# Narrowing float64 weights: the low three bits from ScalarE instead of VectorE

## The chip, the cores and the metric

One core of a Trainium2 chip runs the whole program in one launch. The metric is the device time of that core in microseconds (us), taken as the median of several runs.

## The reference

The reference computes attention, then two gated layers (MoE 1 and MoE 2), in float32 from float32 q, k and v and weights given in float64:

```python
# attention: q, k, v of (4, 8, 576, 64); pooled by 4 tokens, plus a band |i - j| < 4
x = out_up + out_local                      # 2304 tokens x 512
x = (sigmoid(x @ w_gate) * (x @ w_val)) @ w_out      # 512 -> 1536 -> 512
h = x @ w_in                                         # 512 -> 2048
out = (h * tanh(softplus(h))) @ w2_out               # 2048 -> 512
```

The weights arrive as 8-byte float64 words. The kernel has to turn each into a float32 word before it can use it.

## The kernel before, in words

The work runs batch by batch (four batches of 576 tokens). `block(b, extra)` (L910) lays out the matrix products of MoE 1 for batch b, and `weave` (L792) puts the steps of the weights, of the next batch's attention and of the MoE 2 weights among them, each when its due time on a TensorE clock has come. The first batch is different: its attention steps stand in an order written out by hand (`ORDER`, L20 to L30), with the engine of each step in `ENG` (L32 on). A scheduler then fixes the order of the instructions on each engine. After the fourth batch MoE 2 follows (L1051 on).

TensorE multiplies in pairs of float32r words: every float32 operand is split by `split` (L189) into a high part (ScalarE, L190) and a low part (POOL for the first batch's weights, VectorE for others, L191). The products of MoE 1 are at L857 to L859 (gate and value) and L888 to L892 (out), those of MoE 2 at L1060 to L1062 and L1068 to L1070. `m1` evaluates the gate with a tanh on ScalarE (L862) and a product on VectorE (L863).

The weights of MoE 1 come in 18 units of two pieces each. For batch 0 a piece is loaded raw as 128 x 512 float64 words by `load64` (L169; SP queue, L171; two buffers of the tag "raw"), made float32 by `narrow` (L176), and split. A narrowed unit lies in a tile `d` (two buffers) and is also written to DRAM (`wd`, L228 and L256), from where the later batches load it ready-made (L219). Units 0 to 2 are steps of the hand-written order (`wf`, `wn`, `ws`); the others go through `part` (L242), each load being put behind the step of the piece before. The 32 pieces of the MoE 2 weights go through `narrow_steps` (L944) during batches 1 to 3, into a single-buffered tile `d2`.

So `narrow` runs 36 times in the first batch and 32 times later. For one piece it does this:

- L178, ScalarE: the high word of each float64, read as a float32, times 2^-112, into `g` ("rebias"). It subtracts the exponent bias and keeps the 11 lower exponent bits and the top 20 bits of the fraction in place.
- L180, VectorE: `d = g << 3`.
- L181, VectorE: `d = (low word >> 29) | d`, the last three fraction bits.
- L185, VectorE: `d = (g & sign bit) | d`.

L181 is the last reader of the raw buffer, L185 the last reader of `g`, and L180 the first writer of `d`. Attention's own rows that appear below are L98 (copies), L414 (evictions of transposed tokens), L481 and L605 (exponentials), L586 (mask), L636 (normalisation), L648 and L664 (transposes and products), L674 (joining the two attentions).

Of the kernel before, what the change touches and what calls it, by code (L numbers as in the profile page):

```python
# [9 lines left out]
F32R = mybir.dt.float32r  # L10
I32 = mybir.dt.int32
AF = mybir.ActivationFunctionType
ALU = mybir.AluOpType
# [3 lines left out]
SIGN = -2147483648  # L17
# the first batch's loads and steps in the order of their issue
ORDER = [['k0a', 'k0c', 'k1a', 'k1c', 'q0a', 'q0c', 'v1a', 'v1c', 'w0', 'q1c', 'v0c', 'w2', 'v0a',
# [11 lines left out]
# the engines of those steps, and how far apart the second batch's steps are laid (ns)  # L31
ENG = {'L.t0': 3000, 'L.t': 420, 'L.vd': 3750, 'L.vd0': 1800, 'L.pool': 1600, 'L.ls': 4500, 'L.s1':  # L32
# [16 lines left out]
def attn_moe_kernel(  # L49
# [13 lines left out]
    PE, DVE, ACT, POOL, SP = nc.tensor, nc.vector, nc.scalar, nc.gpsimd, nc.sync  # L63
# [18 lines left out]
    scale = 1.0 / float(D) ** 0.5  # L82
# [3 lines left out]
    def subs(b):  # L86
        """The two parts of the tokens of batch b that the products of MoE 1 take in turn."""
        a = 2 * TQ if b == 0 else SUB
        return slice(0, a), slice(a, S)
# [10 lines left out]
    class Step:  # L100
        """A piece of a program: what emits it, the time it takes of the tensor engine, and
        what has to lie how far back on the tensor engine's clock."""

# [3 lines left out]

    # ---------------------------------------------------------------- memory
    const = ctx.enter_context(tc.tile_pool(name="const", bufs=1, side="left"))
# [19 lines left out]
    xl = R[:, OX + NX:OX + 2 * NX].rearrange("p (c t) -> p c t", c=KD)  # L129
    # the products of MoE 1 come to lie where the first batch's rows are gone  # L130
    first = tc.alloc_tile_pool(name="first", bufs=1, side="left", reuse_waits="tile")
# [12 lines left out]
    for n in range(B * NU1):  # L144
        i = n % NRING
        slot_of[n] = (OR + i * 2048, user.get(i))
        user[i] = n
    last = slot_of[B * NU1 - 1][0]
# [18 lines left out]

    # ------------------------------------------------- float64 words to float32
    def load64(src, n):  # L169
# [6 lines left out]
    def narrow(r, d):  # L176
        g = fpool.tile([128, 512], F32, tag="rebias", name="rebias")
        ACT.activation(out=g, in_=r[:, :, 1].bitcast(F32), func=AF.Copy, scale=2.0 ** -112)  # L178
        gi, di = g.bitcast(I32), d.bitcast(I32)
        DVE.tensor_scalar(out=di, in0=gi, scalar1=3, scalar2=None, op0=ALU.logical_shift_left)  # L180
        DVE.scalar_tensor_tensor(  # L181
            out=di, in0=r[:, :, 0], scalar=29, in1=di,
            op0=ALU.logical_shift_right, op1=ALU.bitwise_or,
        )
        DVE.scalar_tensor_tensor(  # L185
            out=di, in0=gi, scalar=SIGN, in1=di, op0=ALU.bitwise_and, op1=ALU.bitwise_or
        )
# [4 lines left out]

    # ------------------------------------------------------- weights of MoE 1
    def src1(u, x):
# [14 lines left out]
    def weights(b):  # L209
        """The steps that bring the units of block b on chip and split them."""  # L210
        steps = []
# [74 lines left out]

    # ------------------------------------------------------------- attention
    class St:
        pass

    def windows(i):
        """Of tile i: first query, first key, first row used and rows used, for its halves."""
        q0, n = tiles[i]
        got = []
        for z in range(2):
            want, m = q0 + z * QH, min(QH, n - z * QH)
            first = min(want, S - WK)
            got.append((first, min(max(want - 3, 0), S - WK), want - first, m))
        return got

    def attention(b):
# [42 lines left out]

        # the first batch's rows lie where the products of MoE 1 come later, four neighbouring
        # tokens of half the sequence to a partition
        def load_rows(src, nm, half, a):
# [108 lines left out]

        # pooled attention, half the queries at a time; heads in the order (parity, pair)
        def g_scores(qh, h0):
# [37 lines left out]

        # the same for half of the pairs, with the transposes
        def f_norm(qh, p0):
# [66 lines left out]

        # banded attention, two windows of 64 queries by 64 keys at a time
        def l_scores(i, e):
# [224 lines left out]
    def weave(slots, steps):  # L792
        """Emits the slots in their order, and the steps among them: each once what it stands
        on lies far enough back, and the paced ones evenly by cost."""
        slots, steps = list(slots), list(steps)
        total_s = sum(z.cost for z in slots) or 1.0
        total_e = sum(z.cost for z in steps if z.paced) or 1.0
        at_s = at_e = 0.0

        def ready(z):  # L800
            t = 0.0
            for name, lat in z.deps:
                if name not in done_at:
                    return None
                t = max(t, done_at[name] + lat)
            return t

        while slots or steps:
            pick, soonest = None, None
            for z in steps:  # L810
                t = ready(z)
                if t is None:
                    continue
                if t <= clock[0]:
                    if z.cost and z.paced and slots and at_e / total_e > (ENG["PACE"] if ("slot", 0, NU1 - 1) not in done_at else 1.15) * at_s / total_s + 0.01:
                        continue
                    pick = z
                    break
                soonest = t if soonest is None else min(soonest, t)
            if pick is None and slots:  # L820
                t = ready(slots[0])
                if t is not None and t <= clock[0]:
                    pick = slots.pop(0)
                    at_s += pick.cost
                elif t is not None:
                    soonest = t if soonest is None else min(soonest, t)
            elif pick is not None:
                steps.remove(pick)
                if pick.paced:
                    at_e += pick.cost  # L830
            if pick is None:
                assert soonest is not None
                clock[0] = soonest
                continue
            pick.fn()
            clock[0] += pick.cost
            done_at[pick.name] = clock[0]

    # ----------------------------------------------------------------- MoE 1
    late = []  # L840
# [5 lines left out]
    def m1(b, f, sub):  # L846
# [13 lines left out]
        sg = fpool.tile([128, SUBM], F32, tag="sg", name="sg")  # L860
        # sigmoid(a) = (1 + tanh(a / 2)) / 2; the last half comes with the second product
        ACT.activation(out=sg[:, 0:n], in_=ps[0][:, 0:n], func=AF.Tanh, scale=0.5)  # L862
# [12 lines left out]
    def m1out(b, c2, fg, j, ps):  # L875
# [19 lines left out]
        if fg == last_g:  # L895
            if b == B - 1 and c2:
                # the ring is free but for its last unit
                a = free_at[j // 2] + j % 2 * 1024
                t = R[:, a:a + 2 * n].rearrange("p (z t) -> p z t", z=2)
            else:  # L900
                t = stage(n)
# [8 lines left out]
    def block(b, extra):  # L910
        """MoE 1 of batch b with the steps of `extra` woven in."""
        slots = []
# [27 lines left out]

    # ------------------------------------------------------- weights of MoE 2
    w2raw = {}

    def narrow_steps(tag, srcs, first, use, gap):  # L944
        """Steps that turn the pieces `srcs` (source, rows) to float32 and hand them to `use`,
        one each `gap` from `first` on."""
        steps = []
# [23 lines left out]
    if True:  # L971
        make_identity(nc, ident)
        POOL.memset(mask, 0.0)
        # row r of a half and column j: queries lie 0 or 3 keys after their window's first
        for z, offs in enumerate(((0, 3), (3, 3), (3, 0))):
# [71 lines left out]

        # ------------------------------------------------------------- MoE 2
        at.release()
# [21 lines left out]

        # tanh(softplus(h)) = n / (n + 2) = n/2 * exp(-ln(n/2 + 1)) with n = e^h (e^h + 2);
        # from h = 10 on it is 1 in float32, and the minimum keeps n in range
        tc.keep_in_program_order(ACT.preload_act_table_set("natural_log_exp_and_others"))
# [30 lines left out]
        for t in range(NT2):  # L1105
# [17 lines left out]
            if t > 0:  # L1123
                for a in range(2):
                    finish(t - 1, po[a], a, full)
        # the last tile's output comes in pieces, so that little is left behind the last product
        for a, cs in ((0, full), (1, slice(0, DM // 2)), (1, slice(DM // 2, DM))):
# [38 lines left out]
```

## Time and profile before

| what | value |
|---|---|
| runs, median of 3 | 1075.83 us (1075.07 to 1077.99) |
| profiled execution, span from its first to its last instruction | 1069.6 us |
| TensorE (PE) busy | 1023.1 us, 96% |
| VectorE (DVE) busy | 690.6 us, 65% |
| ScalarE (ACT) busy | 521.3 us, 49% |
| POOL busy | 195.2 us, 18% |
| moved by DMA | 134.51 MB, mean 126 GB/s |

The span leaves out what lies ahead of the first instruction and behind the last; the profiled execution has no time of its own beside the span, so the span is set against the median of the runs, which is 6.2 us more. The shares are averages over very different stages: POOL has nearly all of its work in the first quarter, and VectorE is far busier there than later. In rows of instructions a number in square brackets is the idle time of the engine just before, with what ended it.

### The profile page before, as it was taken

What the parts mean: (1) busy time and instruction counts of PE and PEld (TensorE: products, weight loads), DVE (VectorE), ACT (ScalarE), POOL (GpSimd) and SP (SyncE); (2) the same over time, 40 slices, a digit from 0 to 9 for tenths busy, and PEclk for the clock granted to TensorE, in tenths of its full rate; (3) what the DMA queues carried; (4) which work ended last, traced back from release to release, by engine and by line L of the source; (5) the groups of instructions that cost most, each with busy time, mean ns of one, the idle gap of its engine ahead of it and who ended that gap; (6) DMA issues with size and microseconds to landing.
All of it is one profiled execution on the core that took longest, in us unless ns stands there. A gap on an engine that the chain in (4) does not pass through costs nothing.

```text
span 1069.6 us, 20453 instructions
## 1 busy us (share of the span) xinstructions
PE 1023.1 (96%) x8152; PEld 956.0 (89%) x8152; DVE 690.6 (65%) x1107; ACT 521.3 (49%) x1222; POOL 195.2 (18%) x235
## 2 busy tenths in 40 slices
PE   4698988999999999999999999999999999999998
PEld 3588978899999999899999999999999999999997
DVE  6977988856975537955488931867555555555552
ACT  4654657346665437565356631654443443433432
POOL 6456564630400400400000002000000000000000
PEclk9998998999999999999999999999999999999999
DMA  8639665777752457622375548212112020220001
GB/s 199 174 103 238 178 204 189 220 241 237 220 184 60 135 179 227 212 101 61 124 243 182 173 167 264 65 29 59 23 37 60 1 60 5 56 60 1 21 1 40
DMA packets 122240, 134.51 MB, mean 126 GB/s; under 512 B 54432, under 2 KB 99488, under 8 KB 122144
## 3 DMA queue, kind: packets, MB, share of 16 engines
q1 hardware_dynamic: 110336, 115.37, 35.1%
q0 software_dynamic: 11808, 17.83, 6.2%
q8 instruction: 64, 1.05, 0.4%
q14 instruction: 32, 0.26, 0.1%
HBM read 101.19 MB, written 31.98 MB: 124 GB/s over the span
## 4 chain that ended last, share of the span: by engine, by line
PE 77%; DVE 11%; DMA 6%; ACT 3%; issue 2%; SPq 0%; POOL 0%; DVEq 0%; ACTq 0%
PE ps_m L857 7%; PE ps_m L859 7%; PE ps_m L858 7%; PE h L1060 6%; PE h L1062 6%; PE h L1061 6%; PE po L1070 6%; PE po L1068 6%; PE po L1069 6%; PE ps_o L888 5%; PE ps_o L890 4%; PE ps_o L892 4%; DVE d L181 2%; DMA raw<-in_moe_w_out_dram 2%; DVE d L185 2%
## 5 line engine op out<-in xcount | busy, mean ns | idle before, releaser
L857 PE MATMUL ps_m<-R 128*128 128x288 f32 (+2 forms) x768 | 236.0, 309 | 4.2 <-DVE sg L863 4.2
L858 PE MATMUL ps_m<-R 128*128 128x288 f32 (+2 forms) x768 | 232.5, 303 | 0.8 <-POOL R L191 0.8
L859 PE MATMUL ps_m<-R 128*128 128x288 f32 (+2 forms) x768 | 232.7, 303 | 0.5 <-POOL R L191 0.5
L857 PEld LDWEIGHTS ps_m<-R 128*128 128x128 f32 x768 | 148.4, 194 | 9.6 <-DVE sg L863 4.6
L190 ACT CAST R<-d 128x512 fp32r<-128x512 f32 (+1 forms) x192 | 108.6, 583 | 89.2 <-PE ps_o L890 34.4
L858 PEld LDWEIGHTS ps_m<-R 128*128 128x128 f32 x768 | 148.8, 194 | 1.9 <-POOL R L191 1.0
L859 PEld LDWEIGHTS ps_m<-R 128*128 128x128 f32 x768 | 148.6, 194 | 1.7 <-POOL R L191 0.9
L191 DVE TENSOR_TENSOR R<-d,R 128x512 fp32r<-128x512 f32 (+1 forms) x158 | 105.5, 682 | 55.1 <-ACT R L190 52.9
L888 PE MATMUL ps_o<-G,R 128*128 128x288 f32 (+2 forms) x384 | 116.5, 303 | 0.0
L890 PE MATMUL ps_o<-G,R 128*128 128x288 f32 (+2 forms) x384 | 114.4, 298 | 0.0
L892 PE MATMUL ps_o<-G,R 128*128 128x288 f32 (+2 forms) x384 | 114.2, 298 | 0.0
L1068 PE MATMUL po<-R,G 128*128 128x512 f32 (+1 forms) x247 | 94.5, 383 | 0.0
L1069 PE MATMUL po<-R,G 128*128 128x512 f32 (+1 forms) x247 | 94.0, 381 | 0.0
L1070 PE MATMUL po<-R,G 128*128 128x512 f32 (+1 forms) x247 | 93.5, 383 | 0.0
L1081 ACT ACTIVATE e<-e 128x1024 f32<-128x1024 f32 (+1 forms) x48 | 40.6, 846 | 107.2 <-DVE e L1080 107.2
L1062 PE MATMUL h<-R 128*128 128x256 f32 x320 | 90.2, 282 | 0.0
L1061 PE MATMUL h<-R 128*128 128x256 f32 x320 | 90.2, 282 | 0.0
L1060 PE MATMUL h<-R 128*128 128x256 f32 x320 | 90.2, 282 | 0.0
L1080 DVE TENSOR_SCALAR e<-h 128x1024 f32<-128x1024 f32 (+1 forms) x48 | 45.9, 956 | 58.3 <-PE h L1062 58.1
L178 ACT ACTIVATE rebias<-raw 128x512 f32<-128x512 f32 x68 | 46.0, 677 | 59.8 <-DMA raw<-in_moe_w_out_dram 23.5
L888 PEld LDWEIGHTS ps_o<-G,R 128*128 128x128 f32 x384 | 72.9, 190 | 1.2
L890 PEld LDWEIGHTS ps_o<-G,R 128*128 128x128 f32 x384 | 73.0, 190 | 0.1
(126 smaller groups left out, 2290.3 us busy)
## 6 DMA issues: line engine op xcount, KB each, us to landing
d<-wd SPq DMA_DIRECT2D x54, 512.0 KB
raw<-in_moe_w_out_dram SPq DMA_DIRECT2D x28, 512.0 KB
wd<-d SPq DMA_DIRECT2D x18, 512.0 KB
wd<-R SPq DMA_DIRECT2D x32, 256.0 KB
raw<-in_moe_w_in_dram SPq DMA_DIRECT2D x16, 512.0 KB
x2d<-R SPq DMA_DIRECT2D x24, 288.0 KB
R<-wd POOLq DMA_DIRECT2D x13, 512.0 KB, 6.9
raw<-in_moe_w_gate_dram SPq DMA_DIRECT2D x12, 512.0 KB
```

The source lines that it names most:

```text
L857: PE.matmul(p[:, 0:n], lhsT=wh, rhs=xh[:, c, ts], start=(c == 0), stop=False)
L858: PE.matmul(p[:, 0:n], lhsT=wh, rhs=xl[:, c, ts], start=False, stop=False)
L859: PE.matmul(p[:, 0:n], lhsT=wl, rhs=xh[:, c, ts], start=False, stop=(c == KD - 1))
L888: PE.matmul(p[:, 0:n], lhsT=hi[:, o:o + 128], rhs=gt[:, f, 0, ts], start=(f == 0), stop=False)
L890: PE.matmul(p[:, 0:n], lhsT=hi[:, o:o + 128], rhs=gt[:, f, 1, ts], start=False, stop=False)
L892: PE.matmul(p[:, 0:n], lhsT=lo[:, o:o + 128], rhs=gt[:, f, 0, ts], start=False, stop=(f == KF1 - 1))
L1060: PE.matmul(o, lhsT=wi[:, 0, c, cs], rhs=x[:, 0, c, :], start=(c == 0), stop=False)
L1061: PE.matmul(o, lhsT=wi[:, 0, c, cs], rhs=x[:, 1, c, :], start=False, stop=False)
L1062: PE.matmul(o, lhsT=wi[:, 1, c, cs], rhs=x[:, 0, c, :], start=False, stop=(c == KD - 1))
L1068: PE.matmul(p, lhsT=g[:, 0, ts], rhs=w[:, 0, cs], start=(j == 0), stop=False)
L1069: PE.matmul(p, lhsT=g[:, 0, ts], rhs=w[:, 1, cs], start=False, stop=False)
L1070: PE.matmul(p, lhsT=g[:, 1, ts], rhs=w[:, 0, cs], start=False, stop=(j == KF2 - 1))
```

## The change

A second ScalarE instruction makes the low three bits. It reads one byte of each float64, the highest byte of the low word, computes byte / 32 + 1 / 64 - 1 / 2 and writes it as an int32 into `d`; the conversion rounds to the nearest whole number, which is byte >> 5. VectorE then does `d = (g << 3) | d` and, as before, `d = (g & sign bit) | d`. L180 is gone, L181 no longer reads the raw words, and the first writer of `d` and the last reader of the raw buffer are now one ScalarE instruction. The remaining hunks of the diff only take away comments.

```diff
+U8 = mybir.dt.uint8
...
     def narrow(r, d):
         g = fpool.tile([128, 512], F32, tag="rebias", name="rebias")
         ACT.activation(out=g, in_=r[:, :, 1].bitcast(F32), func=AF.Copy, scale=2.0 ** -112)
         gi, di = g.bitcast(I32), d.bitcast(I32)
-        DVE.tensor_scalar(out=di, in0=gi, scalar1=3, scalar2=None, op0=ALU.logical_shift_left)
+        ACT.activation(
+            out=di, in_=r.bitcast(U8)[:, :, 3], func=AF.Copy, scale=1.0 / 32, bias=1.0 / 64 - 0.5
+        )
         DVE.scalar_tensor_tensor(
-            out=di, in0=r[:, :, 0], scalar=29, in1=di,
-            op0=ALU.logical_shift_right, op1=ALU.bitwise_or,
+            out=di, in0=gi, scalar=3, in1=di, op0=ALU.logical_shift_left, op1=ALU.bitwise_or
         )
         DVE.scalar_tensor_tensor(
             out=di, in0=gi, scalar=SIGN, in1=di, op0=ALU.bitwise_and, op1=ALU.bitwise_or
         )
```

## Rows read from the trace of the kernel before

**Rows 1.** Stages: stretch, length, busy us of PE, PEld, DVE, ACT, POOL; granted clock, DMA.
```profile
0.00:28.00 28.00, 13.28 (x128) 10.59 (x128) 18.77 (x39) 12.32 (x37) 17.61 (x44) 1.00 0.85 200
28.00:60.00 32.00, 24.00 (x214) 20.64 (x215) 29.83 (x49) 17.85 (x55) 13.17 (x12) 1.00 0.72 197
60.00:220.00 160.00, 144.89 (x1379) 134.34 (x1378) 134.57 (x217) 89.97 (x270) 101.16 (x104) 0.94 0.63 184
220.00:1070.00 850.00, 840.93 (x6435) 790.42 (x6433) 507.48 (x804) 401.14 (x864) 63.30 (x77) 1.00 0.35 110
```

**Rows 2.** Chain that ended last, 28 to 220 us, shares of the stretch by line.
```profile
by line: DVE d L181 8.9%; DVE d L185 7.7%; DMA raw<-in_moe_w_val_dram 6.8%; DVE d L180 6.5%; issue 5.8%; DMA raw<-in_moe_w_out_dram 5.5%; PE ps_m L858 4.2%; PE ps_m L859 4.0%; PE ps_m L857 4.0%; DMA raw<-in_moe_w_gate_dram 3.8%; DMA vw<-in_
```

**Rows 3.** TensorE's timeline: start, length, instruction, wait before it with what ended it.
```profile
42.66 1.96 PE L664 MATMUL ps_la<-ETl,vw 64*64 64x58 f32 x32 [1.86 <-ACT ETl L97]
...
97.99 1.12 PE L579 MATMUL ps_l<-kT,qT 64*64 64x64 f32 x16 [2.35 <-ACT qT L414]
...
176.69 0.50 PE L555 MATMUL ps_ga<-ETg,vd 72*64 72x72 f32 x2 [2.21 <-DVE El L586]
...
198.94 1.14 PE L664 MATMUL ps_la<-ETl,vw 64*64 64x58 f32 x32 [1.73 <-issue]
...
219.18 0.63 PE L648 MATMUL ps_lt<-ident,El 128*128 128x128 f32 x4 [2.15 <-DVE El L636]
...
291.34 0.40 PE L857 MATMUL ps_m<-R 128*128 128x288 f32 x1 [1.93 <-DVE sg L863]
```

**Rows 4.** A short stretch behind one of those waits, columns as in rows 1.
```profile
98.00:104.80 6.80, 6.80 (x40) 6.16 (x40) 4.00 (x9) 5.97 (x24) 5.29 (x9) 0.51 1.07 262
```

**Rows 5.** VectorE's groups at L180, to 60, 60 to 220, after 220 us.
```profile
L180 DVE TENSOR_SCALAR d<-rebias 128x512 int32<-128x512 int32 x6 | 6.5, 1078 | 0.3 <-ACT rebias L178 0.3
...
L180 DVE TENSOR_SCALAR d<-rebias 128x512 int32<-128x512 int32 x30 | 21.5, 720 | 13.4 <-ACT rebias L178 7.9 <-POOL R L191 4.1 <-issue 1.3
...
L180 DVE TENSOR_SCALAR d<-rebias 128x512 int32<-128x512 int32 x32 | 17.4, 543 | 2.0 <-ACT rebias L178 1.8
```

**Rows 6.** Shortest, median and longest of a kind (ns); the last gives its mean.
```profile
L180 DVE TENSOR_SCALAR d<-rebias x68: 409/426/2216, 30.8 to 609.2; 128x512 int32<-128x512 int32 x68
...
L178 ACT ACTIVATE rebias<-raw x68: 652/676/705, 30.1 to 605.4; 128x512 f32<-128x512 f32 x68
...
L190 ACT CAST R<-d x34: 601/618/647, 35.4 to 217.5; 128x512 fp32r<-128x512 f32 x34
...
L1081 ACT ACTIVATE e<-e 128x1024 f32<-128x1024 f32 (+1 forms) x48 | 40.6, 846 | 107.2 <-DVE e L1080 107.2
```

**Rows 7.** SP queue's waits to 225 us: total, times, longest.
```profile
SPq L171 <- DVE d L181: 70.4, 26, 7.7
```

**Rows 8.** One piece's timeline, from its rebias to the next load into its raw buffer.
```profile
37.16 0.67 ACT L178 ACTIVATE rebias<-raw 128x512 f32<-128x512 f32 x1 [1.08 <-DMA raw<-in_moe_w_gate_dram]
...
40.05 0.69 DVE L181 SCALAR_TENSOR_TENSOR d<-raw,d 128x512 int32<-128x512 int32 x1
...
40.82 0.37 SPq L171 DMA_DIRECT2D raw<-in_moe_w_gate_dram  x1
```

**Rows 9.** VectorE's timeline at three places ahead of TensorE's waits.
```profile
93.85 2.95 DVE L185 SCALAR_TENSOR_TENSOR d<-rebias,d 128x512 int32<-128x512 int32 x1
...
173.48 1.50 DVE L180 TENSOR_SCALAR d<-rebias 128x512 int32<-128x512 int32 x1
...
290.51 0.41 DVE L180 TENSOR_SCALAR d<-rebias 128x512 int32<-128x512 int32 x1
```

**Rows 10.** ScalarE's timeline at two places.
```profile
96.83 0.62 ACT L190 CAST R<-d 128x512 fp32r<-128x512 f32 x1 [3.23 <-DVE d L185]
...
209.78 0.67 ACT L178 ACTIVATE rebias<-raw 128x512 f32<-128x512 f32 x1 [3.53 <-DMA raw<-in_moe_w_out_dram]
```

**Rows 11.** POOL's timeline at unit 15's second split.
```profile
211.96 1.28 POOL L191 TENSOR_TENSOR R<-d,R 128x512 fp32r<-128x512 f32 x1
```

**Rows 12.** VectorE's waits to 225 us: total, times, longest.
```profile
DVE d L180 <- POOL R L191: 4.1, 1, 4.1
```

## The prediction

> **What bounds the kernel now.** I read the stages first [rows 1]. TensorE is busy 840.93 of 850 us after 220 us: there it is the bound, and work on VectorE or ScalarE can hide. Before that it stands idle for 14.7 us (to 28), 8.0 us (28 to 60) and 15.1 us (60 to 220). The first narrowing starts at 30 us [rows 6], so the first 14.7 us are out of the change's reach. From 60 to 220 us the granted clock is 0.94 in the mean: 0.06 x 160 = 9.6 us of TensorE time are lost to it. One of four such falls shows where: right behind the 2.35 us wait that ends at 97.99 [rows 3] the granted clock is 0.51 for 6.8 us [rows 4], the lower of its two levels (1.2 GHz instead of 2.4), which costs half of that, 3.4 us. So at most 8.0 + 15.1 + 9.6 = 32.7 us can be won before 220 us.
>
> Next the chain of waits over these 192 us [rows 2]. The three narrowing lines of VectorE hold 8.9 + 7.7 + 6.5 = 23.1% of it, L180 alone 6.5%, or 12.5 us; raw weight loads hold 6.8 + 5.5 + 3.8 = 16.1%, or 31 us; the three MoE 1 products only 12%. VectorE is busy 29.8 of 32 and 134.6 of 160 us, ScalarE 17.9 and 90.0 [rows 1]. So the early stage hangs on VectorE's queue and on the ring of raw loads behind it, and ScalarE has room in the mean. The reader should see in TensorE's timeline [rows 3] that its waits are for attention steps (a mask, a copy, a normalisation) that stand in VectorE's or ScalarE's queue behind narrowing, rarely for weights themselves.
>
> **The change, part by part.** *VectorE loses L180.* In the first batch that is 6 of 1.078 and 30 of 0.720 us, 6.5 + 21.5 = 28.0 us; later 32, 17.4 us [rows 5]. Its shortest is 0.409, its longest 2.216 us [rows 6]: the surplus is waiting that falls into the instruction, so the 36 are worth between 36 x 0.409 = 14.7 and 28.0 us. L181 only gets another input of the same size; I take its duration as unchanged.
>
> The rows show L180 drawn out to 1.50 us at 173.48, and L185, which stays, to 2.95 us at 93.85 [rows 9]; so what draws one out can also draw out the other. I therefore use neither total for the gain, but credit it below wait by wait. The Trainium skill's page "SBUF — State Buffer", section "Who interferes with whom", speaks against the larger number: VectorE and GpSimd hold one shared port pair exclusively for a whole instruction, and an instruction with two SBUF inputs is blocked as well, so the wait would pass from L180 to its successor. L185's 2.95 us agrees with that; by the rule VectorE is relieved of 14.7 us, by the rows' means of 28.0.
>
> *ScalarE gains one instruction per piece.* Its kind (byte in, int32 out) is not in the trace. The nearest row is L178: same 512 elements, same distance of 8 bytes, same function, 0.676 us [rows 6]. A plain cast of as many neighbouring words takes 0.618, one of 1024 elements 0.846 [rows 6]; that bounds it. I take 0.676, or 36 x 0.676 = 24.3 us in the first batch (22.2 to 30.5). ScalarE's 120.1 us of the first 220 become 144, 66%. The 32 later ones, 21.6 us, hide behind TensorE at 99% with ScalarE at 401 of 850; without that cover they would cost up to their 21.6 us.
>
> *A piece's own latency grows.* VectorE's first operation now needs both ScalarE results: with idle engines 0.676 takes the place of 0.409, 0.27 us more per piece. This is covered while the raw loads are waited for.
>
> *The raw buffer comes free sooner.* The load queue waits 70.4 us in 26 waits for L181 [rows 7]. For one piece rebias starts at 37.16, L181 ends at 40.74 and the load goes out at 40.82 [rows 8]. Now the second ScalarE instruction ends at 37.16 + 2 x 0.676 = 38.5, so the load can leave 2.3 us sooner. SP's queue is in order, so the token and value loads behind it move up too; no DMA is added. What is late next is then ScalarE or POOL's split.
>
> *The first write of d moves to ScalarE.* Its wait for the buffer goes with it; priced among the rivals.
>
> *What of this reaches TensorE.* 28 to 60 us: the load that leaves 2.3 us sooner feeds the piece behind which the next attention steps queue, and the wait of 1.86 us at 42.66 [rows 3] is for a copy behind a narrowed piece: I credit 2.5 of the 8.0 us idle, less than the two together (4.2) because ScalarE is nearly without gaps around 30 to 36 us. 60 to 220 us: the wait before 97.99 comes of L185's 2.95 us, which held a ScalarE cast for 3.23 us [rows 9, 10] and a copy behind it; both operations of that piece would now be through before, worth 2.35 + 3.4 with the clock, of which I credit 3.5. The wait before 176.69 ends in a mask operation behind L180's 1.50 us: 1.0 of 2.21. Before 219.18 two L180 stand in the way: 1.0 of 2.15. Before 198.94, 0.7 of 1.73; for all others together 1.3. That is 7.5 us, 0.27 of the 28.0 us taken from VectorE. The ScalarE instructions delay what stands behind them: 30 x 0.676 = 20.3 us, about half of it while ScalarE is busy (90 of 160 us), and at the same 0.27 it costs 2.7, say 2.5 us. After 220 us: twice, before 291.34 and once more near 442, TensorE waits for a gate product that stands right behind an L180 of 0.41 us [rows 3, 9]: 0.7 us. Sum: -2.5 - 7.5 + 2.5 - 0.7 = **-8.2 us**, span 1069.6 to 1061.4; the median of the runs lies 6.2 us above the span, so 1075.8 - 8.2 = **1067.6 us**.
>
> **Rivals.** *Larger gain.* With the loads sooner and VectorE relieved, the long waits go and the clock stays up from 60 to 220 us: 9.6 + 7.5 + 2.5 + 0.7 = 20 us without the ScalarE charge, and with part of it 1055 to 1062, middle 1059. For it: the falls stand behind waits of one to two and a half microseconds. Against: VectorE and POOL stay the same crowded pair.
>
> *No change.* What draws L180 out beyond its shortest only passes to the next VectorE operation, so the relief is 14.7 instead of 28.0 us and the credit 7.5 x 14.7 / 28.0 = 3.9 us; with the early 2.5 halved and ScalarE's charge at its upper bound (2.5 x 30.5 / 24.3 = 3.1) about -2.8 is left: 1073 to 1078, middle 1075. Against: L180's share of the chain. The Trainium skill's rule on the shared port pair ("SBUF — State Buffer", "Who interferes with whom") comes out here.
>
> *Slower: the write in place stops ScalarE.* The byte instruction needs a free d buffer, and thus POOL's split of the unit two back. Before, VectorE waited for that once, 4.1 us [rows 12], at unit 17: its rebias ended at 210.45, the split at 213.24 [rows 10, 11], so ScalarE would stand 2.8 us, with tanh, exponentials and evictions behind it. As loads come 2.3 us sooner, other units get there too. Three such waits of 2 us on TensorE, each with a fall of the clock (9.6 us over four falls, 2.4 each), are 3 x 4.4 = 13.2; less half of the gain, 4, this gives +9, 1085. It decides once ScalarE reaches a unit's byte instruction over 1 us before POOL is through. Against: only one such wait so far.
>
> The order of each queue is the scheduler's and may come out differently; a few microseconds either way, within these ranges.
>
> **How the numbers follow.** About 0.3%, 3.2 us, can be told from no change. Forecast 0.45 (1062 to 1072.6), larger gain 0.17, no change 0.15, slower 0.23. Faster 0.45 + 0.17 = 0.62, same 0.15, slower 0.23. The range takes in the larger gain down to 1057 and the slower case up to 1083; beyond lie some 0.06 and 0.11. The likeliest case's own range is 1062 to 1073.
>
> **What would show it.** Right: L180's group gone, the byte instruction near 0.68 us; SP's waits for VectorE at L171 gone and much less than 70 us left; VectorE's busy time to 220 us down by 15 to 28 us; TensorE idle from 28 to 220 us down from 23.1 to some 17 us, and fewer falls of the clock. Wrong: L185 and its neighbour growing by as much as L180 gave up (no change); ScalarE waiting for POOL ahead of the byte instruction, and TensorE's waits now put down to ScalarE (slower); or a byte instruction well over 0.85 us.

## The result, and the profile after

The changed kernel takes 1082.55 us (median of 4 runs, 1081.76 to 1085.68) against 1075.45 us for the kernel before: a ratio of 1.0092, 95% interval 1.0066 to 1.0118. It is slower by 0.9%, where 0.8% faster was forecast. The profiled execution took 1083.0 us, with a span of 1081.2 us, 11.6 more than before. Lines from `narrow` on stand 4 further down: rebias L179, the byte instruction L183, VectorE's two operations L186 and L189, the casts L194, POOL's split L195.

TensorE's busy time rose from 1023.1 to 1028.0 us, and its idle time from 1069.6 - 1023.1 = 46.5 to 1081.2 - 1028.0 = 53.2. So 6.7 of the 11.6 us are waits and 4.9 are the same products taking longer. The stages of the changed kernel, with the columns of [rows 1], show where:

```profile
0.00:28.00 28.00, 13.28 (x128) 10.59 (x128) 18.11 (x39) 11.66 (x33) 16.82 (x43) 1.00 0.86 193
28.00:60.00 32.00, 24.99 (x235) 21.39 (x237) 27.60 (x53) 24.38 (x76) 14.90 (x15) 1.00 0.75 207
60.00:220.00 160.00, 147.85 (x1369) 137.08 (x1370) 115.77 (x178) 102.71 (x289) 99.81 (x104) 0.90 0.61 178
220.00:240.00 20.00, 12.90 (x98) 12.51 (x97) 5.01 (x9) 6.75 (x13) 5.51 (x6) 0.74 0.78 244
220.00:1081.00 861.00, 841.88 (x6424) 790.06 (x6422) 493.93 (x771) 418.63 (x895) 60.74 (x76) 0.99 0.36 109
```

What the change was to bring did come. VectorE is busy for 18.1 + 27.6 + 115.8 = 161.5 us to 220 us, 21.7 less than in [rows 1]; TensorE's idle time from 28 to 220 us fell from 23.1 to 7.0 + 12.2 = 19.2 us. But the granted clock of 60 to 220 us went from 0.94 to 0.90, and the stretch behind it, where TensorE had not waited, now has 7.1 us of idle time in 20, and a clock of 0.74. Before, that stretch was:

```profile
220.00:240.00 20.00, 20.00 (x172) 19.72 (x171) 9.47 (x15) 7.95 (x17) 6.59 (x7) 1.00 0.78 256
```

VectorE's two remaining operations from 60 to 220 us, behind the two that they replace, and SP's waits to 225 us (total, times, longest), answer to [rows 5, 7]:

```profile
L185 DVE SCALAR_TENSOR_TENSOR d<-rebias,d 128x512 int32<-128x512 int32 x30 | 28.9, 968 | 0.3
L181 DVE SCALAR_TENSOR_TENSOR d<-raw,d 128x512 int32<-128x512 int32 x30 | 26.3, 882 | 0.2
...
L189 DVE SCALAR_TENSOR_TENSOR d<-rebias,d 128x512 int32<-128x512 int32 x30 | 28.4, 958 | 0.2
L186 DVE SCALAR_TENSOR_TENSOR d<-rebias,d 128x512 int32<-128x512 int32 x30 | 26.3, 884 | 13.7 <-ACT d L183 13.5 <-ACT rebias L179 0.2
```

```profile
SPq L172 <- ACT d L183: 39.2, 15, 14.7
SPq L260 <- DVE d L189: 24.5, 7, 4.9
SPq L329 <- POOL vd L432: 13.9, 7, 3.9
```

Three of TensorE's waits between 90 and 240 us (start, length, instruction, and in brackets the wait before it):

```profile
95.41 0.68 PE L583 MATMUL ps_l<-kT,qT 64*64 64x64 f32 x16 [1.91 <-ACT qT L418]
...
154.06 1.16 PE L668 MATMUL ps_la<-ETl,vw 64*64 64x58 f32 x32 [1.97 <-ACT od L565]
...
230.30 1.96 PE L668 MATMUL ps_la<-ETl,vw 64*64 64x58 f32 x32 [7.10 <-ACT ETl L98]
```

At each the clock fell, right behind the first two and during the third, as it did behind the wait of [rows 4], but for longer. The columns are those of [rows 1]:

```profile
96.70:106.90 10.20, 9.35 (x49) 8.47 (x49) 6.53 (x12) 8.91 (x30) 5.29 (x6) 0.52 1.06 239
154.70:175.20 20.50, 20.50 (x127) 18.18 (x124) 10.17 (x22) 9.10 (x25) 3.72 (x4) 0.51 0.47 150
226.40:236.60 10.20, 6.30 (x50) 6.20 (x51) 3.07 (x6) 5.52 (x12) 2.50 (x2) 0.52 0.87 315
```

The 7.10 us wait is new, and two timelines tell how it comes about. First ScalarE, then SP:

```profile
227.41 0.66 ACT L179 ACTIVATE rebias<-raw 128x512 f32<-128x512 f32 x1 [9.73 <-DMA raw<-in_moe_w_out_dram]
...
229.66 0.59 ACT L98 COPY ETl<-ps_lt 128x512 f32<-128x512 f32 x1
```

```profile
213.50 7.38 SPq L329 DMA_DIRECT2D araw<-in_v_dram  x4
220.97 0.83 SPq L172 DMA_DIRECT2D raw<-in_moe_w_out_dram  x2
```

The copy that TensorE needs stands behind the rebias of the first MoE 2 piece; that rebias waits 9.73 us for its raw load; and the raw loads stand on SP's queue behind four loads of attention values, which wait in turn for POOL to free their buffer. Nothing of this is `narrow`. In the kernel before, the raw loads went out at 215.90 and the same copy ran at 221.94 us:

```profile
215.90 0.95 SPq L171 DMA_DIRECT2D raw<-in_moe_w_out_dram  x2
...
221.94 0.58 ACT L97 COPY ETl<-ps_lt 128x512 f32<-128x512 f32 x1
```

The order on the queues had changed, and not only here. The program hands its work to the scheduler in the same order as before, yet of the instructions that both kernels have, some 60 of SP's 369, 160 of TensorE's 7320, 160 of ScalarE's 1020 and 190 of VectorE's 1039 stand elsewhere, by the two lists that the last experiment writes out. So two theories stood against each other: **A**, the loss comes from the new order of the queues; **B**, it comes from the new instruction on ScalarE itself.

### The profile page after: what moved, and what is told of

Its sections match the earlier page's. It is cut to its first block, busy times and chain, and to the rows that moved or that the text cites. A ratio compares the mean times of both kernels' runs of the same rounds, so it can differ in the third digit from the quotient of the medians.

```text
span 1081.2 us, 20349 instructions
## 1 busy us (share of the span) xinstructions
PE 1028.0 (95%) x8152; PEld 959.1 (89%) x8152; DVE 655.4 (61%) x1039; ACT 557.4 (52%) x1290; POOL 192.3 (18%) x235
## 4 chain that ended last, share of the span: by engine, by line
PE 71%; DMA 10%; DVE 8%; ACT 6%; issue 3%; POOL 1%; SPq 0%; ACTq 0%; DVEq 0%; POOLq 0%
PE h L1064 6%; PE h L1066 6%; PE h L1065 6%; PE po L1074 6%; PE po L1072 6%; PE po L1073 6%; PE ps_o L892 5%; PE ps_m L861 5%; PE ps_o L894 4%; PE ps_o L896 4%; PE ps_m L863 4%; PE ps_m L862 4%; DMA raw<-in_moe_w_in_dram 4%; DVE R L195 2%; PE ps_la L668 1%
## 5 line engine op out<-in xcount | busy, mean ns | idle before, releaser
L194 ACT CAST R<-d 128x512 fp32r<-128x512 f32 (+1 forms) x192 | 109.2, 582 | 87.1 <-PE ps_o L894 36.4
L195 DVE TENSOR_TENSOR R<-d,R 128x512 fp32r<-128x512 f32 (+1 forms) x158 | 104.8, 677 | 64.5 <-ACT R L194 61.6
L186 DVE SCALAR_TENSOR_TENSOR d<-rebias,d 128x512 int32<-128x512 int32 x68 | 55.4, 818 | 36.9 <-ACT d L183 36.3
L179 ACT ACTIVATE rebias<-raw 128x512 f32<-128x512 f32 x68 | 45.7, 673 | 60.3 <-DMA raw<-in_moe_w_out_dram 24.3
L892 PEld LDWEIGHTS ps_o<-G,R 128*128 128x128 f32 x384 | 73.1, 190 | 1.3
```

Of the source, the lines that this page charges most:

```text
L892: PE.matmul(p[:, 0:n], lhsT=hi[:, o:o + 128], rhs=gt[:, f, 0, ts], start=(f == 0), stop=False)
```

## Experiments

To hold an order, each instruction of a queue gets an issue-order edge (no wait) behind the one that precedes it in a given list. This is the edit that most of the kernels below share; they differ in the operations of `narrow` and in the list.

```diff
+        for names in QUEUES:
+            for prev, z in zip(names, names[1:]):
+                tc.add_manual_dep(
+                    traced[z], prev,
+                    mybir.DependencyInfo(mybir.DependencyClass.NoSync, mybir.DependencyReason.DATA),
+                    reason="order",
+                )
```

Ratios below are to runs of the kernel before on the same chip.

**The new operations in the old order.** The list is that of the kernel before; the byte instruction stands directly behind its rebias in the first batch (one piece excepted), and later where the old order first allows it.

> The changed narrowing, but every queue held to the order of the kernel before (issue order alone, no added wait); the byte instruction stands directly behind its rebias in the first batch except for unit 17's first piece, and later where the old order first allows it. Theory A (the loss comes from the new order that the scheduler gave the queues): the work itself gains, so faster than the kernel before, 1064 to 1073 us. Theory B (the loss comes from the byte instruction on ScalarE, in whatever order): as slow as the changed kernel, 1080 to 1086 us, with ScalarE ahead of TensorE's waits. If neither part matters: 1073 to 1078 us.

Measured: 1069.92 us, ratio 0.9963 (0.9939 to 0.9987). The same instructions that made the kernel slower make it faster in the old order, by about 4 us (by the interval 1.4 to 6.6). This is also the version that beats both kernels. Its stages, columns as in [rows 1]:

```profile
28.00:60.00 32.00, 24.96 (x233) 21.76 (x233) 27.83 (x51) 22.15 (x65) 14.75 (x14) 1.00 0.73 201
60.00:220.00 160.00, 146.89 (x1429) 137.22 (x1430) 118.48 (x185) 107.99 (x306) 102.77 (x109) 0.95 0.68 197
220.00:240.00 20.00, 20.00 (x152) 19.98 (x151) 8.19 (x15) 7.36 (x16) 1.09 (x1) 1.00 0.70 221
```

TensorE is busy for about as long to 220 us as in the changed kernel, but at 0.95 instead of 0.90, and without a gap from 220 to 240 us. Theory B, as the whole cause, falls.

**The old operations in the new order.** The mirror of it: the three VectorE operations of before, every queue in the changed kernel's order.

> The old narrowing (three VectorE operations, no byte instruction), every queue held to the order of the changed kernel. Theory A: slow, 1080 us or more, with the wait of some 7 us for an eviction behind a late raw load near 230 us still there. Theory B: like the kernel before, 1073 to 1078 us.

Measured: 1116.47 us, ratio 1.0386 (1.0346 to 1.0426). TensorE's longest waits (total, times, longest), the 7.7 us being the place of 230 us, which this slower run reaches at 251:

```profile
PE ps_la L668 <- ACT ETl L98: 13.9, 3, 7.7
PE ps_m L862 <- POOL R L195: 12.4, 1, 12.4
```

The new order costs the old operations 3.9% and the new ones 1.0092 - 0.9963 = 1.3%. It fits the new operations better than the old, as an order laid for them should, and is worse for both than the order of before.

**The byte instruction added, nothing taken away.** Order of before, all three VectorE operations kept; L181 and L185 do the real work, and the byte is overwritten.

```diff
+        ACT.activation(
+            out=di, in_=r.bitcast(U8)[:, :, 3], func=AF.Copy, scale=1.0 / 32, bias=1.0 / 64 - 0.5)
         DVE.tensor_scalar(out=di, in0=gi, scalar1=3, scalar2=None, op0=ALU.logical_shift_left)
```

> The old narrowing and, besides, the byte instruction into the same buffer d ahead of it (its result is overwritten), in the order of the kernel before: ScalarE's cost alone. Theory A: 0 to +5 us, 1075 to 1081 us. Theory B: +7 us or more, 1082 us or more, at least the whole loss since VectorE is not relieved.

**The shift left out.** Order of before; L180 is gone and nothing takes its place, so the weights lack their shift.

```diff
-        DVE.tensor_scalar(out=di, in0=gi, scalar1=3, scalar2=None, op0=ALU.logical_shift_left)
         DVE.scalar_tensor_tensor(
-            out=di, in0=r[:, :, 0], scalar=29, in1=di, op0=ALU.logical_shift_right, op1=ALU.bitwise_or
+            out=di, in0=r[:, :, 0], scalar=29, in1=gi, op0=ALU.logical_shift_right, op1=ALU.bitwise_or
         )
```

> The left shift by three (L180) is left out and nothing put in its place, so the weights come out wrong; order of the kernel before: VectorE's relief alone, without ScalarE's cost. By the prediction's terms 10.7 us (2.5 + 7.5 + 0.7) less, 1065 us; if what draws L180 out only passes to its neighbour, 1070 to 1074 us; if the relief reaches nothing, 1075 us. Theory A and B say the same here.

Measured: 1086.12 us, ratio 1.0118 (1.0079 to 1.0157), for the byte added; 1061.86 us, ratio 0.9904 (0.9869 to 0.9938), for the shift left out. 60 to 220 us, the first line with the byte added, the second with the shift left out (its profile is of the fastest of its six runs, 1054.72 us, so its clock of 0.98 is better than its mean):

```profile
60.00:220.00 160.00, 143.14 (x1331) 133.00 (x1331) 127.42 (x208) 101.07 (x280) 94.65 (x100) 0.90 0.60 177
```

```profile
60.00:220.00 160.00, 148.15 (x1470) 138.79 (x1471) 123.48 (x190) 94.11 (x280) 102.19 (x109) 0.98 0.72 207
```

Taking L180 away is worth 0.0096 x 1074 = 10.3 us (6.7 to 14.1). Adding the byte instruction by itself costs 12.7 us, which is what theory B had forecast for this run, and well over theory A's 0 to 5 us. The run does not decide between them, for here VectorE's shift (L183 in this kernel) has to wait for the byte instruction as well, since both write the same tile: 18.3 us from 60 to 220 us, where [rows 5] have 7.9 us of waits for ScalarE.

```profile
L183 DVE TENSOR_SCALAR d<-rebias 128x512 int32<-128x512 int32 x29 | 19.6, 679 | 18.3 <-ACT d L181 18.3
```

The kernel with the new operations in the old order is the one with the shift left out, with the byte instruction put in. So that instruction's price in its real place is 0.9963 - 0.9904 = 0.0059, or 6.3 us (by the two intervals some 2 to 11). It is not free, but by the middles less than the relief.

**The place at 230 us.** Three kernels in the changed kernel's own order, with one or both of these moves:

```diff
 SP queue
+raw<-in_moe_w_out_dram  x2
 araw<-in_v_dram  x4
-raw<-in_moe_w_out_dram  x2
```

```diff
 ScalarE queue
+ETl<-ps_lt
 rebias<-raw
 ...
-ETl<-ps_lt
```

> The changed kernel in its own order, with one move in SP's queue: the first two raw loads of the MoE 2 weights go ahead of the four token loads (araw) that wait for POOL. Theory A, in its narrow form (one misplaced pair of loads costs the 7.1 us wait at 230 us and the fall of the clock behind it, 5.1 us): 1069 to 1074 us, and TensorE idle under 2 us between 220 and 240 us. If the loss is spread over the whole order: 1078 to 1083 us. Theory B (ScalarE's instruction itself): 1080 us or more.

> The changed kernel in its own order, with one move in ScalarE's queue: the eviction (copy ETl) that TensorE waits for at 230 us goes ahead of the rebias that waits for the late raw load; SP's queue is as it was. Narrow form of theory A: 1069 to 1075 us although the raw load is as late as before. Loss spread over the order: 1078 to 1083 us. Theory B: 1080 us or more.

> The changed kernel in its own order, with the two moves of the runs before made together: on the queue of SyncE the two first raw loads of the second MoE stage stand ahead of the four araw loads, and on ScalarE the copy of ETl stands ahead of the rebias that waits for those loads. If the loss against the order of before sat in this one place, both moves together would bring the kernel to 1070 us, the time that the new operations have in the old order. If the place is only one of several, the time stays near what the eviction's move alone gave, 1076 to 1080 us, with no wait of over 4 us between 215 and 240 us, and the rest of the loss in the clock's falls between 96 and 200 us.

Measured: loads first 1084.91 us, ratio 1.0077 (1.0048 to 1.0105), copy first 1078.35 us, 1.0050 (1.0020 to 1.0080), both 1080.63 us, 1.0058 (1.0031 to 1.0086). The profiles of the first two are of the quickest and the third quickest of twelve runs, 1074.21 and 1072.79 us. In them the wait shrinks from 7.1 to 4.1 us with the loads first, and is gone with the copy first:

```profile
220.00:240.00 20.00, 19.23 (x164) 18.88 (x164) 7.50 (x14) 8.42 (x16) 2.54 (x2) 1.00 0.86 277
```

With both moves a new wait comes up near the same place, and the four value loads wait longer still on SP. TensorE's and SP's timelines of that kernel:

```profile
225.89 0.66 PE L892 MATMUL ps_o<-G,R 128*128 128x344 f32 x1 [3.42 <-DVE R L907]
...
211.82 0.89 SPq L172 DMA_DIRECT2D raw<-in_moe_w_out_dram  x2
212.81 9.22 SPq L329 DMA_DIRECT2D araw<-in_v_dram  x4
```

By the middles of the intervals the place is worth some 4 us (1.0092 to 1.0050); the intervals overlap, so this is not sharp. For none of the three did the time come to the 1069 to 1075 us that a single bad place would have given, and of the two forecasts for both moves the one for one place of several (1076 to 1080 us, no wait over 4 us) is near: this wait is one of several losses.

**A later due time for the MoE 2 pieces.** Here the scheduler is left free. Does another due time clear the place, and what does it do to the kernel before?

```diff
-                    ("o2", b), srcs, clock[0] + 1000.0,
+                    ("o2", b), srcs, clock[0] + 9000.0,
```

> The changed kernel with one number of its plan changed, the due time of the first MoE 2 weight load (1000 to 9000 ns behind the second batch's start); the scheduler lays its queues anew. Theory A: the place at 230 us is relieved, some 1070 to 1076 us, unless the new order has a bad place of its own; in any case not the 1082.6 us by necessity. Theory B: 1080 us or more.

> The kernel before with the same number changed: how far such a shift of the plan moves a kernel without the change. Theory A: it can move by several us either way, 1068 to 1085 us, since the order is drawn anew. Theory B: 1073 to 1078 us.

Measured: the changed kernel 1080.23 us, ratio 1.0076 (1.0049 to 1.0102), the kernel before 1073.37 us, ratio 1.0003 (0.9977 to 1.0029). The wait for the copy is still there in the changed kernel, 6.1 us. The due time does not govern it, and this led no further.

**Half of each order.** The new operations, with one order up to a cut near 140 us and the other behind it.

```diff
-QUEUES = new
+QUEUES = [z for z in old if z in ahead] + [z for z in new if z not in ahead]
```

```diff
-QUEUES = new
+QUEUES = [z for z in new if z in ahead] + [z for z in old if z not in ahead]
```

> The changed operations; every queue in the order of before up to a cut, and from there in the order of the changed kernel. The cut is about 140 us into the profile: all work that the first 180 VectorE instructions need. If the loss arises behind the cut (the wait of 7 us at 230 us and the fall of the clock at it), the time is that of the changed kernel, 1080 to 1083 us. If it arises ahead of the cut (the falls at 97 and 155 us), the time is that of the new operations in the old order, 1070 us. If it is spread, 1075 to 1078 us. A new order that is only right for its own beginning would give waits just behind the cut.

> The mirror of the run with the old order first: every queue in the order of the changed kernel up to the cut at about 140 us, and from there in the order of before. If the loss arises behind the cut, 1070 us, and no wait of over 4 us behind 200 us; if ahead of it, 1080 to 1083 us with the fall of the clock near 97 us as in the changed kernel; if spread, 1075 to 1078 us.

Measured: old then new 1085.63 us, ratio 1.0115 (1.0083 to 1.0147); new then old 1073.03 us, ratio 1.0005 (0.9982 to 1.0027). The second is the clean one. Its stages around the cut:

```profile
60.00:140.00 80.00, 71.59 (x645) 65.85 (x645) 53.25 (x92) 49.16 (x140) 48.45 (x54) 0.91 0.64 170
140.00:220.00 80.00, 76.37 (x748) 71.75 (x748) 59.80 (x94) 56.48 (x159) 50.52 (x51) 0.97 0.68 207
220.00:240.00 20.00, 20.00 (x164) 19.72 (x164) 7.49 (x12) 7.25 (x14) 5.16 (x6) 0.95 0.68 212
```

With the old order behind the cut, 0.87% of the 1.29% come back: by the middles the greater part of the loss arises behind 140 us, and 0.42% is left. (The forecast of no wait over 4 us behind 200 us did not hold; there is one of 5.60 us for ScalarE's tanh near 446 us, of which more below.) The other half has a wait of its own just behind the seam, so its time tells less about the new order than its ratio seems to:

```profile
154.32 1.23 PE L474 MATMUL ps_g<-kd,qd 64*72 64x144 f32 x4 [8.51 <-ACT ETg L548]
...
232.93 1.96 PE L668 MATMUL ps_la<-ETl,vw 64*64 64x58 f32 x32 [5.37 <-ACT ETl L98]
```

**The edges themselves.** Each kernel with its own order written out.

```diff
+QUEUES = own order of this kernel
```

> The changed kernel, with nothing changed but that its own order of every queue is written out by the same issue-order edges that the other runs use. If the edges themselves cost nothing, it gives the time of the changed kernel, 1082 us, within 2 us; and over its runs the granted clock lies near 0.978, so that some 23 us are lost to the clock and 1057 to 1059 us are left (the changed kernel's four runs have 23.8 and 1057.6). If the edges cost or save time, it lies elsewhere, and the comparisons of orders are off by as much. If the clock of four runs was chance, the share lost to it comes nearer to the 11.6 us of the kernel before.

> The kernel before, with nothing changed but that its own order of every queue is written out by the same issue-order edges. If the edges cost nothing, no difference from the kernel before (ratio within 0.002 of 1), with some 12 us lost to the clock. If they save time, the gain of the new operations in the old order (4 us) is the edges' and not the operations'.

Measured: the changed kernel 1084.04 us, ratio 1.0103 (1.0065 to 1.0142), the kernel before 1075.69 us, ratio 1.0018 (0.9996 to 1.0039). The edges save nothing; if anything they cost 0.1 to 0.2%. So the gain in the old order is the operations', not the edges'. The changed kernel's held order has the wait of 230 us again, 6.8 us of idle time in 20, but from 60 to 220 us this run's clock was 0.94, as in [rows 1], and not 0.90:

```profile
60.00:220.00 160.00, 149.57 (x1392) 139.37 (x1392) 115.42 (x181) 103.23 (x292) 99.56 (x106) 0.94 0.61 178
220.00:240.00 20.00, 13.21 (x108) 12.82 (x107) 4.90 (x9) 6.81 (x13) 5.26 (x5) 0.83 0.81 254
```

So the wait belongs to the order, while where and how long the clock falls differs between runs of one order, and one profile does not tell it. Means over many runs do. Each run has a mean granted clock; span times (1 - clock) estimates the TensorE time that it took away (with what fell into idle time counted in). Over the 93 runs of the kernel before that stand beside the experiments the mean is 11.6 us, leaving 1060.0 of the span. The ten runs in the changed kernel's order (four free, six held) lose 21.9 us and leave 1059.8. The twelve with the new operations in the old order lose 13.8 and leave 1054.1. So the new order takes back the 6 us that the operations save outside the clock, and some 8 us of clock on top; with ten runs each of these is good to 3 or 4 us.

## Why the prediction was wrong

**The step that failed** is the sentence that the scheduler's order "may come out differently; a few microseconds either way, within these ranges". The order alone is worth 1.29% of 1074, or 13.8 us (by the two intervals some 10 to 18), more than every other term. I built the sum on the old timeline, wait by wait, as if each instruction would stay where it was. None of the three rivals had the order as its cause. The slower rival's time, 1085 us, was near the one measured, and 1082.55 lies within the range, but that is luck: the sign of the forecast was wrong, and in the changed kernel the rival's mechanism is not what costs the time.

**VectorE's relief: right in its sum.** 21.7 us less busy time, within 15 to 28. The sum credited 2.5 + 7.5 + 0.7 = 10.7 us for it; the shift left out, in the old order, gave 10.3 us. Its parts came out otherwise: of the early 2.5 us nothing is to be seen, TensorE's idle time from 28 to 60 us being 7.9 us there against 8.0 before. The rival by which L180's surplus only passes on to the next operation did not come about: L186 takes 884 ns and L189 958 from 60 to 220 us, where L181 took 882 and L185 968. From the Trainium skill's rule on the port pair ("SBUF — State Buffer", "Who interferes with whom") the prediction had inferred that the two would grow. In the changed kernel they did not; with the shift left out a little of it shows, 990 and 953 ns, or 93 of L180's 720 ns.

**The byte instruction's length: right.** 0.676 us was taken, and the shortest, median and longest are (ns):

```profile
L183 ACT ACTIVATE d<-raw x68: 644/668/702, 31.3 to 622.6; 128x512 int32<-128x512 uint8 x68
```

**ScalarE's charge: too small by the middles, and looked for in the wrong place.** The sum had 2.5 us, all of it in the first batch; the 32 later byte instructions were to hide behind TensorE. In the old order, with L180 gone, the instruction costs 6.3 us (2 to 11, so the size alone does not refute 2.5). The longer latency of a piece is not what it pays for: with the shift left out VectorE's first operation waits 7.5 us for ScalarE from 60 to 220 us, with the new operations in the old order 8.1 us.

```profile
L186 DVE SCALAR_TENSOR_TENSOR d<-raw,rebias 128x512 int32<-128x512 int32 x31 | 30.6, 990 | 9.5 <-ACT rebias L179 7.5 <-POOL R L195 2.0
```

```profile
L186 DVE SCALAR_TENSOR_TENSOR d<-rebias,d 128x512 int32<-128x512 int32 x31 | 26.1, 844 | 10.6 <-ACT d L183 8.1 <-DMA raw<-in_moe_w_out_dram 2.4
```

In the profiles of these two kernels TensorE's idle time from 28 to 220 us is nearly the same, 19.8 us without the byte instruction and 20.2 us with it. From 240 to 1050 us it is 4.2 us without and 11.7 us with it. There TensorE waits for the gate (total, times, longest); the lines are the kernel before, the shift left out, and the new operations in the old order:

```profile
PE ps_m L857 <- DVE sg L863: 4.2, 2, 2.2
...
PE ps_m L861 <- DVE sg L867: 1.8, 2, 1.3
...
PE ps_m L861 <- ACT sg L866: 9.7, 2, 5.6
```

ScalarE, ahead of the longer of the last two waits, and then that wait of TensorE:

```profile
440.31 0.67 ACT L183 ACTIVATE d<-raw 128x512 int32<-128x512 uint8 x1 [4.30 <-DVE R L195]
440.89 0.39 ACT L866 ACTIVATE sg<-ps_m 128x288 f32<-128x288 f32 x1
...
441.33 0.61 PE L861 MATMUL ps_m<-R 128*128 128x288 f32 x1 [5.60 <-ACT sg L866]
```

The byte instruction of a MoE 2 piece is the first to write the single buffer `d2`, so it waits until VectorE's split has read the piece before; the tanh stands behind it on ScalarE, and TensorE waits for the tanh. From 220 to 620 us ScalarE stands so for 29 of the 32 pieces:

```profile
ACT d L183 <- DVE R L195: 23.9, 29, 4.3
```

The two waits for the tanh come again in the other two kernels that have the byte instruction in the old order behind 220 us: 9.0 us with the byte added, 8.4 us with the new order first and the old behind it. So by these profiles what ScalarE is charged for is mainly the write in place, at a buffer and an engine that the prediction did not look at, and not the 0.27 share of the instructions' length that the sum used. It was not tested further: no run gave `d2` a second buffer, or put the byte instruction behind the tanh. The 10.3 and 6.3 us add up to the 4.0 measured because the 6.3 is their difference; that is no separate check.

**The raw buffer: right.** SP's wait for it fell from 70.4 to 39.2 us, and all waits of the raw loads together from 80.0 to 65.5 us. The longest single one, 14.7 us, is longer than before.

**The write in place: not the cause of the loss.** The slower rival wanted ScalarE held by POOL's split ahead of the byte instruction. In the changed kernel ScalarE's waits there over the whole span, in us and times, are:

```profile
  DVE R L195: 8.4, 6
  POOL R L195: 1.9, 2
  DMA wd<-d: 1.5, 1
```

Two waits for POOL of 1.9 us in all do not make three of two with a fall of the clock each. The first line is VectorE's split of the MoE 2 pieces: 8.4 us in 6 waits, where the old order has 23.9 us in 29, and TensorE's waits for the tanh behind 220 us are 1.7 us in this kernel. So in the scheduler's new order the write in place costs little, while in the old order it is, by these profiles, the main price of the change.

**Fewer falls of the clock: wrong.** TensorE's waits from 28 to 220 us did shrink, but in the profiled run the falls grew longer, and over ten runs in this order the clock took 21.9 us, not 11.6.

**What stays open.** Why the scheduler lays SP's and ScalarE's queues otherwise when one VectorE instruction turns into a ScalarE one was not traced; a later due time did not change it. Nor is the loss behind 140 us assigned place by place: the wait at 230 us is worth some 4 us of it, and the rest, as well as what arises ahead of 140 us, was not broken up. That the falls follow from the waits is read from where they stand; no run held the clock while keeping a wait.

## What to carry to other kernels

Where a scheduler fixes the order of the queues, an edit to one helper is two changes: the operations, and a new order of everything. Before believing either sign, hold the old order and run the new operations in it; here that separated -4 from +10 us. Look first at the instructions that got a new neighbour on a queue, not at the ones that were edited: TensorE's longest new wait came of four loads that waited for buffers that the edit never touched. And where an edit moves the first write of a tile to another engine, follow every buffer that it writes: here the prediction followed `d` of the first batch and not `d2`, where in the old order the price lay.

## What the runs showed of the hardware

I had expected a fall of the clock to be short: the one in [rows 4] lasts 6.8 us behind a wait of 2.35 us. In the changed kernel the granted clock stayed at 0.51 for 20.5 us with TensorE busy through all of them, behind a wait of only 1.97 us, and for 10.2 us behind one of 7.10 us. In the rows here the length of a fall does not follow that of the wait. Nor does the order fix it: from 60 to 220 us the mean clock was 0.90 in one run of the changed kernel's order and 0.94 in another.

The runs of one program also spread more than I had assumed: the changed kernel with its order held took between 1078.15 and 1089.11 us in six runs, which is 1.0%, against the 0.3% that the prediction had taken as clear.
